# Projections and FFN as four concurrent 32-column tiles in a two-layer attention kernel

## The chip, the cores and the metric

The kernel runs on one core of one Trainium2 chip. The metric is device time in microseconds (us) of one execution. Runs of one kernel mostly agree within 0.5%, so differences of a few us need several rounds, in which kernels run in turn on the same chip. A ratio here is the mean time of one kernel's fast runs over that of the kernel before in the same rounds, so it is not quite the ratio of the medians that stand beside it. A kernel can also run in a slower state; no run told of here did, and "fast" means no more than that.

Names used below: the page is the profiler's summary of one execution, and the chain in it is the work that ended last, followed back through what each step waited for. ACT is ScalarE, DVE is VectorE, PE is TensorE (PEld its weight loads), POOL is GpSimd. L889 is line 889 of the program that is profiled. Lines move with every edit, so the scores are L1109 before and L1115 after.

## The reference

Two identical layers over 2048 rows of width 512: attention with 32 heads of 16 dimensions, then a feed-forward network (FFN) of width 1792.

```python
x = x + _A_ref(_layernorm(x), wqkv, wo)      # q,k,v = x @ wqkv; softmax(q k^T / 4) v; @ wo
x = x + _B_ref(_layernorm(x), w1, b1, w2, b2)  # gelu(x @ w1 + b1) @ w2 + b2
# ... both once more, with the same weights
```

## The kernel before

The program is made ahead of time by a small list scheduler, which is part of the kernel. Every piece of work is an `_Op` with an engine, a believed cost in us, the buffers it reads and writes, and for PE a `mode`: "S" for scores (weights of 32 rows and 128 columns), "P" for PV products (128 rows, 17 of 32 columns, four tiles side by side), "F" for full-array matmuls. The scheduler keeps a clock for each engine and always takes the piece that can start first; for a change of mode it charges `SW`. No time from the chip reaches it: a program, once made, is fixed.

```python
MM = 0.2135          # believed cost of one matmul of 512 columns
DV = 0.69            # of one VectorE eviction
FQ = 2               # matmuls in one piece of F work
SW = 0.107           # of a change of mode
...
    def _cost(self, op):
        return op.cost + (SW if op.eng == "pe" and op.mode != self.mode else 0.0)
...
# FFN, second matmul (ytile): 14 full-array matmuls and the bias as a 15th, of one row
fns = [lambda e, fc=fc: e.matmul(pb, lhsT=T["G"][:, fc, q], rhs=T["W2"][:, fc, :], start=(fc == 0), stop=False)
       for fc in range(NFC)]
fns.append(lambda e: e.matmul(pb, lhsT=T["ONES1"][0:1, :], rhs=T["B2row"][0:1, :], start=False, stop=True))
for h in range(0, NFC + 1, FQ):
    ...
    yield _Op("pe", FQ * MM, fns[h:h + FQ], reads=..., writes=["B.%d" % b], prio=MID if h else FPRIO)
```

Softmax exponentials are shared between ACT (exponentials of two or three score tiles at a time) and DVE (an approximation in integer arithmetic, which needs four PV products a tile instead of one). Who takes which tile is decided by the same scheduler. Where it expects PE to idle too long it puts in warming matmuls.

The softmax here doesn't subtract the row's maximum and nothing guards it: scores larger than these inputs give would overflow.

## Time and profile before

Before: 1621.02 us (median of 3 runs; 1620.97 with the next three).

| what | number | from |
|---|---|---|
| span of the profiled run | 1619.2 us | the page |
| ACT busy | 1554.1 us, 96% | the page, part 1 |
| PE busy, modelled ends | 1459.1 us, 90% | the page, part 1 |
| PE's slots: each instruction of the program at its measured step | 1375.6 us | starts in the timeline |
| DVE busy | 1363.4 us, 84% | the page, part 1 |
| first exponential starts, last one starts, end | 12.8, 1588.6, 1619.2 us | the timeline of ACT |

A busy share says which engine can be the limit. ACT is, almost without a break, from the first exponential to the last; only then does PE run the last rows' FFN alone. So time can be gained in two ways: less work on ACT, or exponentials that start less late. Two consecutive exponentials start 0.904 us apart (two tiles) or 1.330 us apart (three) where nothing hinders them. Below, a "late start" is one that comes over 60 ns later than that. Before there are 161 of them, worth 63.5 us. What other work of ACT takes between two exponentials is taken off (without the gaps that hold such work it is 148 late starts and 60.4 us). The page's own idle column is smaller, because a recorded ACT instruction overlaps the next one a little (one of three tiles is recorded as 1.52 us long, and the next starts after 1.33).

### The profile page before, as it was taken

To read this page: it belongs to the slowest core of one execution; us is meant where nothing else is said; L and a number is where in the kernel's file an instruction comes from. 1 tells how busy PE (TensorE), PEld (TensorE's weight loads), DVE (VectorE), ACT (ScalarE), POOL (GpSimd) and SP (SyncE) were. 2 spreads that over 40 slices of the span, in tenths; PEclk is the share of its full clock that TensorE was granted. 3 is DMA by queue.
4 is the path that set the end of the run, shared out by engine and by line. 5 is a ranking of instruction groups with operands and counts; after the bars stand their busy time and mean duration, and the time that the engine had idled before them with its cause. 6 is when DMAs were issued, how large, how long until landed. Compare 5 with 4: busy or idle time off the path is not lost.

```text
span 1619.2 us, 33814 instructions
## 1 busy us (share of the span) xinstructions
PE 1459.1 (90%) x14297; PEld 421.7 (26%) x14297; DVE 1363.4 (84%) x2649; ACT 1554.1 (96%) x1396; POOL 111.7 (7%) x148
## 2 busy tenths in 40 slices
PE   8998888989999998999989989878999989889998
PEld 2222222222222222222222222222222222233344
DVE  5689889879988889879798788988879988888993
ACT  7989999989999999999999999999999999999995
POOL 3200000000000000000010000010000000010000
PEclk9999999999999999999999999999999999999999
DMA  6100001101010010101101001001101100011120
GB/s 176 20 1 1 2 14 28 33 8 40 21 40 21 14 40 21 40 14 21 34 24 39 11 15 40 1 1 34 40 14 27 34 14 11 5 41 37 28 77 27
DMA packets 88370, 44.90 MB, mean 28 GB/s; under 512 B 33693, under 2 KB 88222, under 8 KB 88222
## 3 DMA queue, kind: packets, MB, share of 16 engines
q1 hardware_dynamic: 88222, 42.75, 9.9%
q8 instruction: 114, 1.87, 0.5%
q14 instruction: 34, 0.28, 0.1%
HBM read 33.03 MB, written 2.10 MB: 22 GB/s over the span
## 4 chain that ended last, share of the span: by engine, by line
ACT 70%; PE 27%; DVE 2%; issue 1%; DMA 0%; POOL 0%; ACTq 0%; POOLq 0%
ACT pt L1405 58%; PE ps L1466 8%; PE ps L1109 8%; ACT v L1405 5%; ACT kt L1405 4%; ACT g L878 3%; PE ps L889 3%; PE ps L843 2%; PE ps L647 2%; PE ps L644 1%; PE ps L770 1%; ACT L878 1%; ACT L1405 1%; PE ps L1097 1%; DVE du L1254 0%
## 5 line engine op out<-in xcount | busy, mean ns | idle before, releaser
L1405 ACT ACTIVATE pt<-ps 128x1024 bf16<-128x1024 f32 (+1 forms) x1190 | 1308.5, 1255 | 30.9 <-PE ps L1466 14.8
L1109 PE MATMUL ps<-qp,kt 32*128 32x512 bf16 x4096 | 539.4, 385 | 138.4 <-ACT pt L1405 92.8
L1254 DVE TENSOR_SCALAR du<-ps 128x512 uint16<-128x512 f32 x659 | 445.6, 686 | 114.9 <-PE ps L1109 106.8
L1466 PE MATMUL ps<-pt,v 128*17 128x512 bf16 (+1 forms) x3151 | 438.9, 362 | 5.1 <-ACT pt L1405 2.1
L1109 PEld LDWEIGHTS ps<-qp,kt 32*128 32x128 bf16 x4096 | 141.5, 91 | 687.7 <-ACT pt L1405 292.5
L1466 PE MATMUL ps<-du,vc 128*17 128x512 bf16 (+1 forms) x2211 | 308.6, 359 | 1.7 <-DVE du L1317 0.8
L1317 DVE TENSOR_SCALAR du<-du 128x2048 uint16<-128x2048 uint16 x332 | 227.9, 691 | 2.1
L1057 POOL TENSOR_SCALAR qp<-q,mask 128x512 bf16<-128x512 bf16 (+1 forms) x91 | 66.3, 728 | 1291.8 <-PE ps L1109 1282.8
L1466 PE MATMUL ps<-du,v 128*17 128x512 bf16 (+1 forms) x737 | 141.2, 362 | 1.5 <-DVE du L1254 0.6
L1315 DVE TENSOR_SCALAR du<-du 128x1024 uint16<-128x1024 uint16 x332 | 135.3, 417 | 2.4
L1466 PEld LDWEIGHTS ps<-pt,v 128*17 128x17 bf16 x3151 | 105.7, 88 | 120.7 <-issue 86.7
L843 PE MATMUL ps<-xf,wr 128*128 128x512 bf16 (+1 forms) x472 | 123.8, 365 | 0.5 <-DVE g L857 0.2
L889 PE MATMUL ps<-w,g 128*128 128x512 bf16 x448 | 120.4, 382 | 3.5 <-ACT g L878 3.4
L1405 ACT ACTIVATE v<-ps 128x1536 bf16<-128x1536 f32 (+1 forms) x81 | 104.5, 1309 | 4.9 <-PE ps L1466 3.1
L1466 PE MATMUL ps<-dh,vc 128*17 128x512 bf16 (+1 forms) x384 | 108.6, 359 | 0.0
L1466 PEld LDWEIGHTS ps<-du,vc 128*17 128x17 bf16 x2211 | 85.0, 89 | 58.9 <-issue 28.4
L1405 ACT ACTIVATE kt<-ps 128x1536 bf16<-128x1536 f32 (+1 forms) x66 | 93.3, 1420 | 2.3 <-PE ps L1466 1.4
L1254 DVE TENSOR_SCALAR dh<-ps 128x512 uint16<-128x512 f32 x115 | 78.9, 686 | 15.2 <-PE ps L1109 14.1
L857 DVE TENSOR_SCALAR g<-ps,hb1t 128x512 bf16<-128x512 f32 (+1 forms) x112 | 79.9, 713 | 12.3 <-PE ps L843 10.9
L1254 DVE TENSOR_SCALAR kt<-ps 128x512 uint16<-128x512 f32 x100 | 68.3, 683 | 16.1 <-PE ps L1109 14.3
L1466 PE MATMUL ps<-kt,v 128*17 128x512 bf16 (+1 forms) x311 | 77.2, 365 | 0.0
L1097 PE MATMUL ps<-w 128*32 128x512 bf16 x719 | 70.5, 388 | 1.6 <-DVE du L1254 1.6
(86 smaller groups left out, 1206.5 us busy)
## 6 DMA issues: line engine op xcount, KB each, us to landing
wr<-in_B_w_dram SPq DMA_DIRECT2D x59, 256.0 KB, 2.8
wr<-in_A_wqkv_dram SPq DMA_DIRECT2D x24, 256.0 KB, 2.8
wr<-in_A_wo_dram SPq DMA_DIRECT2D x18, 256.0 KB, 3.0
out_dram<-x SPq DMA_DIRECT2D x16, 128.0 KB, 1.7
w<-in_B_w_dram SPq DMA_DIRECT2D x1, 1792.0 KB, 10.9
g<-in_A_wqkv_dram SPq DMA_DIRECT2D x3, 512.0 KB, 5.2
x<-in_A_x_dram SPq DMA_DIRECT2D x3, 512.0 KB, 8.1
kt<-in_B_w_dram SPq DMA_DIRECT2D x4, 256.0 KB, 3.8
```

Of the source, the lines that this page charges most:

```text
L843: fns = [lambda e, dc=dc, j=j, pb=pb: e.matmul(pb, lhsT=T["WR"][w][:, 256 * dc + 128 * j:256 * dc + 128 * j + 128], rhs=T["XF"][:, dc, q], ...
L857: yield _Op("dve", 0.21 + n / 966, lambda e, fc=fc, pb=pb: e.tensor_scalar(T["G"][:, fc, q], pb, T["HB1T"][:, fc:fc + 1], None, op0=ALU.ad ...
L878: lambda e, g=g: e.activation(out=g, in_=g, func=ACT.Gelu_apprx_tanh), reads=gk, writes=gk, prio=2)
L889: fns = [lambda e, fc=fc: e.matmul(pb, lhsT=T["G"][:, fc, q], rhs=T["W2"][:, fc, :], start=(fc == 0), stop=False) for fc in range(NFC)]
L1057: yield _Op("pool", 0.1 + 0.6 * w / 512, lambda e, s=s, q=q, i=i, t=t, w=w: e.tensor_scalar(T["QP"][:, s, w * i:w * i + w], q, T["MASK"][: ...
L1097: fns.append(lambda e, o=o, w=w, a=a, m=m: e.matmul(o, lhsT=w, rhs=rhs, start=start, stop=start, tile_position=(0, m * a)))
L1109: return (lambda e: e.matmul(o, lhsT=lhsT, rhs=rhs, start=True, stop=True, tile_position=(32 * a, 0)), ["K%d.%d.%d" % (l, gb, kt // 4), "Q ...
L1254: yield _Op("dve", 0.68, lambda e: e.tensor_scalar(u, self.bank(b), E_SCALE, E_BIAS, op0=ALU.mult, op1=ALU.add), reads=["B.%d" % b], write ...
L1315: yield _Op("dve", 0.08 + 0.14 * n, lambda e: e.tensor_scalar(U[:, 1, 0:n, :], U[:, 0, 0:n, :], SHIFT, None, op0=ALU.add), reads=key[0], w ...
L1317: yield _Op("dve", 0.08 + 0.28 * n, lambda e: e.tensor_scalar(U[:, 2:4, 0:n, :], U[:, 0:2, 0:n, :], 2 * SHIFT, None, op0=ALU.add), reads=k ...
L1405: yield _Op("act", 0.065 + 0.4267 * n, lambda e, src=src, dst=dst: e.activation(out=dst, in_=src, func=ACT.Exp, scale=0.25), reads=["B.%d" ...
L1466: op.fns.append(lambda e, o=o, lhsT=q[0][0][m], rhs=q[0][1][:, n * m:n * m + n], a=a, st=st, sp=sp: e.matmul(o, lhsT=lhsT, rhs=rhs, start= ...
```

## The change

Intent: full-array matmuls sit between scores and PV products, and each change of tile shape costs PE 0.096 us here (0.311 us from start to start in place of 0.216). This pause is called a drain below. If projections and FFN have the tile shape of PV, one of the shapes is gone. Each full-array matmul becomes four matmuls of 32 columns, with the same moving operand; the one-row bias is padded to 128 rows with zeros.

```diff
+    def quads(self, out, lhsT, rhs, start, stop):
+        return [lambda e, a=a: e.matmul(out[32 * a:32 * a + 32, :], lhsT=lhsT[:, 32 * a:32 * a + 32], rhs=rhs, start=start, stop=stop,
+                                        tile_position=(0, 32 * a)) for a in range(4)]
...
-        fns = [lambda e, fc=fc: e.matmul(pb, lhsT=T["G"][:, fc, q], rhs=T["W2"][:, fc, :], start=(fc == 0), stop=False)
-               for fc in range(NFC)]
-        fns.append(lambda e: e.matmul(pb, lhsT=T["ONES1"][0:1, :], rhs=T["B2row"][0:1, :], start=False, stop=True))
+        fns = []
+        for fc in range(NFC):
+            fns += self.quads(pb, T["G"][:, fc, q], T["W2"][:, fc, :], fc == 0, False)
+        fns += self.quads(pb, T["ONES1"][:, :], T["B2row"][:, :], False, True)
         for h in range(0, NFC + 1, FQ):
             yield ("need", ("g", l, seg, min(h, NFC - 1) // 2))
-            yield _Op("pe", FQ * MM, fns[h:h + FQ],
+            yield _Op("pe", min(FQ, NFC + 1 - h) * MM, fns[4 * h:4 * h + 4 * FQ],
...
-                      writes=["B.%d" % b], prio=MID if h else FPRIO)
+                      writes=["B.%d" % b], prio=MID if h else FPRIO, mode="P")
... the same in proj (Q, K, V), wo and hpair (FFN, first matmul); ONES1 and B2row get 128 rows, zeroed on POOL
```

The edit does two things at once. It changes the shape on the hardware, and it changes what the scheduler believes, through `mode="P"` and through a lower cost for the last piece, which holds the bias alone, so that every later choice comes out differently.

More of the change, by code (lines that the diff above doesn't have):

```diff
@@ L450, in bass_interleave_layers__mha_block__dense_activation_gelu__prompt_kernel @@
         T["B1c"] = sb([NFC, 128], BF16, "b1c")
-        T["B2row"] = sb([1, D], BF16, "b2row")
-        T["ONES1"] = sb([1, 128], BF16, "ones1")
+        T["B2row"] = sb([128, D], BF16, "b2row")
+        T["ONES1"] = sb([128, 128], BF16, "ones1")
         T["ZERO"] = sb([128, 32], BF16, "zero")
@@ L522, in init @@
         yield _Op("pool", 0.1, lambda e: e.memset(T["ZERO"][:], 0.0), writes=["ZERO"])
-        yield _Op("pool", 0.1, lambda e: e.memset(T["ONES1"][:], 1.0), writes=["ONES1"])
+        yield _Op("pool", 0.1, lambda e: e.memset(T["ONES1"][:], 0.0), writes=["ONES1"])
+        yield _Op("pool", 0.1, lambda e: e.memset(T["ONES1"][0:1, :], 1.0), reads=["ONES1"], writes=["ONES1"])
+        yield _Op("pool", 0.3, lambda e: e.memset(T["B2row"][:], 0.0), writes=["B2zero"])
         yield _Op("dve", 0.6, lambda e: e.memset(self.bank(PVB), 0.0), writes=["B.%d" % PVB])
@@ L556, in loads @@
         yield load(T["B1c"][:], hbm["b1"].rearrange("(c p) -> c p", p=128), "db1", ["B1c"], 0.2)
-        yield load(T["B2row"][:], hbm["b2"].rearrange("(o e) -> o e", o=1), "db2", ["B2row"], 0.2)
+        yield _Op("sp", 0.2, lambda e: e.dma_start(T["B2row"][0:1, :], hbm["b2"].rearrange("(o e) -> o e", o=1)),
+                  reads=["B2zero"], writes=["B2row", "B2zero"], sem="db2", by=16, tail=2.0)
         yield load(T["W2"][:], hbm["w2"].rearrange("(c p) e -> p c e", p=128), "dw2", ["W2"], 8.0)
@@ L642, in proj @@
         for dc in range(NDC):
-            if kind == "V":
-                fns.append(lambda e, dc=dc: e.matmul(pb, lhsT=src(dc, i), rhs=wt(dc), start=(dc == 0),
-                                                     stop=(dc == NDC - 1)))
-            else:
-                fns.append(lambda e, dc=dc: e.matmul(pb, lhsT=wt(dc), rhs=src(dc, None),
-                                                     start=(dc == 0), stop=(dc == NDC - 1)))
+            lhsT, rhs = (src(dc, i), wt(dc)) if kind == "V" else (wt(dc), src(dc, None))
+            fns += self.quads(pb, lhsT, rhs, dc == 0, dc == NDC - 1)
         reads = wkeys + (skeys[i % 4:i % 4 + 1] if kind == "V" else skeys)
         for h in range(0, 4, FQ):
-            yield _Op("pe", FQ * MM, fns[h:h + FQ], reads=reads, writes=["B.%d" % b], prio=MID if h else FPRIO)
+            yield _Op("pe", FQ * MM, fns[4 * h:4 * h + 4 * FQ], reads=reads, writes=["B.%d" % b], prio=MID if h else FPRIO, mode="P")
         if l:
@@ L769, in wo @@
         q = slice((t % 4) * 128, (t % 4) * 128 + 128)
-        fns = [lambda e, j=j: e.matmul(pb, lhsT=T["OTN"][:, j, q], rhs=T["WR"][us[j // 2]][:, 512 * (j % 2):512 * (j % 2) + 512],
-                                       start=(j == 0), stop=(j == 3)) for j in range(4)]
+        fns = []
+        for j in range(4):
+            fns += self.quads(pb, T["OTN"][:, j, q], T["WR"][us[j // 2]][:, 512 * (j % 2):512 * (j % 2) + 512], j == 0, j == 3)
         for h in range(0, 4, FQ):
-            yield _Op("pe", FQ * MM, fns[h:h + FQ], reads=["WR.%d" % us[j // 2] for j in range(h, h + FQ)] + ["OTN.%d.%d" % (j, t % 4) for j in range(h, h + FQ)],
-                      writes=["B.%d" % b], prio=MID if h else FPRIO)
+            yield _Op("pe", FQ * MM, fns[4 * h:4 * h + 4 * FQ], reads=["WR.%d" % us[j // 2] for j in range(h, h + FQ)] + ["OTN.%d.%d" % (j, t % 4) for j in range(h, h + FQ)],
+                      writes=["B.%d" % b], prio=MID if h else FPRIO, mode="P")
         for j in range(2):
@@ L842, in hpair @@
             pb = self.bank(b)[:, 0:n]
-            fns = [lambda e, dc=dc, j=j, pb=pb: e.matmul(
-                pb, lhsT=T["WR"][w][:, 256 * dc + 128 * j:256 * dc + 128 * j + 128], rhs=T["XF"][:, dc, q], start=(dc == 0),
-                stop=(dc == NDC - 1)) for dc in range(NDC)]
+            fns = []
+            for dc in range(NDC):
+                o = 256 * dc + 128 * j
+                fns += self.quads(pb, T["WR"][w][:, o:o + 128], T["XF"][:, dc, q], dc == 0, dc == NDC - 1)
             for h in range(0, 4, FQ):
-                yield _Op("pe", FQ * MM * n / 512, fns[h:h + FQ],
+                yield _Op("pe", FQ * MM * n / 512, fns[4 * h:4 * h + 4 * FQ],
                           reads=["WR.%d" % w] + ["XF.%d" % (t % 4) for t in self.tiles(seg)],
-                          writes=["B.%d" % b], prio=MID if h else FPRIO)
+                          writes=["B.%d" % b], prio=MID if h else FPRIO, mode="P")
             yield from self.wdone((l, seg, "1", p), w)
@@ L888, in ytile @@
         q = slice((t % 4) * 128, (t % 4) * 128 + 128)
-        fns = [lambda e, fc=fc: e.matmul(pb, lhsT=T["G"][:, fc, q], rhs=T["W2"][:, fc, :], start=(fc == 0), stop=False)
-               for fc in range(NFC)]
-        fns.append(lambda e: e.matmul(pb, lhsT=T["ONES1"][0:1, :], rhs=T["B2row"][0:1, :], start=False, stop=True))
+        fns = []
+        for fc in range(NFC):
+            fns += self.quads(pb, T["G"][:, fc, q], T["W2"][:, fc, :], fc == 0, False)
+        fns += self.quads(pb, T["ONES1"][:, :], T["B2row"][:, :], False, True)
         for h in range(0, NFC + 1, FQ):
             yield ("need", ("g", l, seg, min(h, NFC - 1) // 2))
-            yield _Op("pe", FQ * MM, fns[h:h + FQ],
+            yield _Op("pe", min(FQ, NFC + 1 - h) * MM, fns[4 * h:4 * h + 4 * FQ],
                       reads=["W2", "ONES1", "B2row"] + ["G.%d.%d" % (f, t % 4) for f in range(h, min(h + FQ, NFC))],
-                      writes=["B.%d" % b], prio=MID if h else FPRIO)
+                      writes=["B.%d" % b], prio=MID if h else FPRIO, mode="P")
         yield _Op("dve", DV, lambda e: e.tensor_tensor(out=T["X"][:, t, :], in0=T["X"][:, t, :], in1=pb, op=ALU.add),
```

## The prediction

> **What bounds the kernel now.** I read the page from the top: busy shares first, then the chain of work that ended last, then the costliest groups of instructions.
>
> ```profile
> span 1619.2 us, 33814 instructions
> ...
> PE 1459.1 (90%) x14297; PEld 421.7 (26%) x14297; DVE 1363.4 (84%) x2649; ACT 1554.1 (96%) x1396; POOL 111.7 (7%) x148
> ...
> ACT 70%; PE 27%; DVE 2%; issue 1%; DMA 0%; POOL 0%; ACTq 0%; POOLq 0%
> ...
> L1405 ACT ACTIVATE pt<-ps 128x1024 bf16<-128x1024 f32 (+1 forms) x1190 | 1308.5, 1255 | 30.9 <-PE ps L1466 14.8
> ```
>
> ScalarE (ACT) carries the softmax exponentials and is busy 96% of the span; only 65 us of it are idle. The chain agrees: 70% ACT. PE's 90% must be discounted, since matmul ends are modelled and overlap; its real occupancy has to come from starts. Reading ACT by stretches, about 8.5 idle us lie in the first 20 us and some 19 us in the last 40, where the final feed-forward runs alone; about 38 us are scattered between. A cheaper PE can win only in that middle and in the tail, unless it also takes work off ACT.
>
> Next, the timeline of TensorE, for what a tile shape and a change of shape cost.
>
> ```profile
> 1322.63 0.83 PE L1097 MATMUL ps<-w,zero 128*17 128x512 bf16 x12
> 1323.28 1.25 PE L1097 MATMUL ps<-w 128*32 128x512 bf16 x20
> ...
> 1505.32 0.40 PE L1109 MATMUL ps<-qp,kt 32*128 32x512 bf16 x4
> 1505.65 1.04 PE L889 MATMUL ps<-w,g 128*128 128x512 bf16 x4
> 1506.62 0.39 PE L1109 MATMUL ps<-qp,kt 32*128 32x512 bf16 x3
> 1506.94 1.04 PE L889 MATMUL ps<-w,g 128*128 128x512 bf16 x4
> ...
> 1596.38 0.39 PE L891 MATMUL ps<-b2row,ones 1*128 1x512 bf16 x1
> 1596.70 0.60 PE L770 MATMUL ps<-wr,otn 128*128 128x512 bf16 x2
> ```
>
> Columns: start, length, engine, line, operands with rows*columns of the weights. The line numbered 1097 holds warming matmuls; its second row is already what the change makes of the projections: 128 rows, 32 columns, four tiles with one moving operand. Twenty of them are five sets: 1.25 us less one latency of 0.38 is 0.87 for four set-to-set steps, 0.217 us each. Starts read one by one give 0.215 to 0.222 for such sets, and 0.216 (0.226 for the second of a burst) for a full-array matmul. So four 32-column tiles cost what one full-array matmul costs, even eight sets on end.
>
> The scores (L1109, 32 rows) and the FFN (L889, 128x128) alternate. From the last FFN start, at about 1505.65 + 3 x 0.22 = 1506.31, to the next score at 1506.62 it takes 0.31 us, where the same shape would take 0.216. Over the whole trace the median from start to start is 0.311 to 0.317 between scores and either other shape, 0.306 to 0.312 between full-array and PV: a switch costs 0.096 us, alike for every pair.
>
> **What the Trainium skill says.** "TensorEngine Tiling (Array Packing)", section Key Properties: changing the tiling mode drains the engine, using another tile of the same mode doesn't. The trace agrees: 0.311 against 0.216 us. The same page's Restrictions say that column tiling disables Fast Weight Load. This could hurt, but in the trace weight loads hide: sets keep 0.216 us with four loads each. "TensorE: Matmul & The Clock Gate", Part 3, models concurrent tiles as one duration plus about 4 ns a further tile; here the starts inside a set are 3 ns apart. Nothing in these says that the array does more work per microsecond in four tiles when all 128 columns were used before.
>
> **The change part by part.** The programs of both kernels are built ahead by a scheduler in the kernel, which charges itself for mode switches; so I counted the built orders of instructions.
>
> Removed and added on PE. The 1496 full-array or bias matmuls become 1496 sets of four; PE rises from 14,297 to 18,750 matmuls with as many weight loads, at no cost in slots by the warming sets above. Issue can follow: in the trace 46 matmuls of 256 columns went by in 12 sets of 0.109 us, 27 ns each, and the new sets ask for only 54 ns each.
>
> Switches fall far less than one would think, from 2709 to 2521. Between full-array and PV there were 198, nearly all gone. But scores need 32-row tiles, and around them a full-array burst only becomes a column-tiled burst: scores to and from anything were 2511 switches and are 2518. So -188 x 0.096 = -18.0 us of PE.
>
> The new order gives part of it back. PV products fall from 7581 to 7533 matmuls but are packed less well: 1774 sets of 512 columns instead of 1752, and 496 of 256 columns instead of 478, so 22 x 0.216 + 18 x 0.109 = +6.7 us. Score groups rise by 12 (+2.6 us), warming sets by 1 (+0.2 us). The last tile of a set starts 9 ns after its first, and now that precedes every switch to scores: about +3.5 us. Sum: -18.0 + 6.7 + 2.6 + 0.2 + 3.5 = -5.0 us of PE occupancy, from 1375.6 to 1370.6 us when every instruction gets its measured slot. PE already had 1619 - 1376 = 243 us of slack; all but the first and last of the sixteen stretches of 256 score tiles need 67 to 91 us of PE and last 89 to 104.
>
> ACT. How exponentials divide between ACT and VectorE is decided by the same scheduler. ACT has 3222 score tiles before and 3236 after; VectorE 874 and 860. ACT's groups of three go from 548 to 552, of two from 789 to 790. Unhindered starts are 1.330 and 0.904 us apart, so ACT gains 4 x 1.330 + 0.904 = +6.2 us, on the bound engine. VectorE loses 14 tiles at about 0.69 + 0.42 us, 15 us that it doesn't need.
>
> What comes back on the path. Between consecutive exponentials I find 161 starts that come over 60 ns later than those spacings, 63.5 us together. In 50 of these (19.2 us) PE did full-array and PV work between two score groups with a switch between; only there does the removal act directly, and at 0.096 us each it is worth at most 4.8 us. I credit 4.8 and take 2 us off for better PE spacing at the start, where the first stretch needs 100.9 us of PE instead of 103.8 in 112.5. In the tail after the last score, the bias matmul of one row is built as a 32-row tile, so it switches twice: 0.32 us before and after, as at 1596.38. Over all rows it doesn't; the tail has three switches instead of nine, and 23.4 us of PE instead of 24.1: -0.7 us.
>
> Sum on the path: +6.2 - 4.8 - 2.0 - 0.7 = -1.3 us, thus 1619.7, called 1620.
>
> **Rivals.** First, PE relief pulls ACT waits in more broadly: if the full 18 us of switches came off the waits before exponentials and ACT's extra work stayed, 1621 - 18 + 6 = 1609. For it: PE is 27% of the chain and is named for most of ACT's waits. Against it: net occupancy falls only 5 us, and two thirds of the late starts have no such switch before them.
>
> Second, detuning. Pacing constants of the scheduler were set for the old order, and its choices differ from the first microseconds on. If late starts grew by a third, 63.5 / 3 = 21 us, it would be 1621 + 6 + 21 = 1648. For it: single late starts of 2 to 4 us occur already. Against it: the inner stretches keep 9 to 26 us of PE slack and the mix of work in each is alike.
>
> Third, tiles with 32 live columns and 128 live rows stall on weights or instruction issue. If each new set took 0.25 instead of 0.216 us, PE would gain 1496 x 0.034 = 51 us, mostly inside 243 us of slack; in the tail 100 sets would show 3.4 us. Perhaps 1635. The warming sets speak against it, though they run at most eight in a row.
>
> **Range and chances.** Net terms are below 7 us each; what I can't work out is the luck of the new order, which I put at 12 us either way, a little more upward. Range 1606 to 1636. Two per cent is 32 us: faster would need half of all middle and tail waits to vanish (3%), slower the second or third rival at full size (4%).
>
> **What would show it.** In the changed trace: ACT busy about 1560 us with 552 and 790 groups; set-to-set spacing 0.216 us for the projection and FFN lines; 0.31 us at the remaining switches; switch count near 2521; PE summed slots 5 us lower; the bias matmul without its 0.32 steps. I am wrong if ACT's late starts move by more than 15 us either way, if new sets are slower than 0.22 us, or if the granted clock leaves 0.994.

## The result, and the profile after

After: 1609.78 us (median of 6 runs, 1607.56 to 1612.44) against 1620.97 us; ratio 0.9939, 95% interval 0.9921 to 0.9956. A repeat on another occasion gave 1610.93 us, ratio 0.9937. The gain is clear of noise and far below 2%.

From the page of the kernel after, parts 1, 4 and 5. The columns of part 5 are busy us and mean ns of one, then the idle us before them and who ended it.

```profile
span 1610.5 us, 42676 instructions
...
PE 1449.3 (90%) x18750; PEld 453.1 (28%) x18750; DVE 1348.8 (84%) x2615; ACT 1559.4 (97%) x1401; POOL 112.5 (7%) x150
...
ACT 69%; PE 29%; DVE 2%; issue 1%; DMA 0%; POOL 0%; SPq 0%; POOLq 0%; ACTq 0%
...
L1411 ACT ACTIVATE pt<-ps 128x1024 bf16<-128x1024 f32 (+1 forms) x1214 | 1331.8, 1253 | 20.7 <-PE ps L1115 10.8
...
L511 PE MATMUL ps<-xf,wr 128*32 128x512 bf16 (+1 forms) x2400 | 169.0, 368 | 0.9 <-DVE g L862 0.3
...
L511 PEld LDWEIGHTS ps<-xf,wr 128*32 128x32 bf16 x2400 | 54.3, 95 | 60.5 <-issue 28.5
```

ACT is busier by 5.3 us (1559.4 against 1554.1) and the kernel is still shorter: ACT has more work and waits less. The idle time before its main group of exponentials fell from 30.9 to 20.7 us. The chain's shares hardly moved, so the bound is the same engine.

Where the time went, by the starts of exponentials in both timelines:

| us | before | after |
|---|---|---|
| to the first exponential | 12.8 | 12.8 |
| first to last exponential | 1575.8 | 1566.9 |
| after the last one's start | 30.6 | 30.8 |
| exponentials between at 0.904 and 1.330 us | 1441.2 | 1447.4 |
| late starts | 161, 63.5 us | 145, 48.3 us |

All of it lies in the middle: 6.2 us more work and 15.2 us less lateness make -9.0, and the stretch is 8.9 us shorter. The tail gained nothing.

The new sets run at the expected speed. One line from the timeline of PE in the tail (start, length, line, weights as rows*columns):

```profile
1600.46 1.89 PE L511 MATMUL ps<-w,g 128*32 128x512 bf16 x30
```

Thirty matmuls are seven and a half sets; 1.89 us less one latency of 0.38 is 1.51 us for seven steps, 0.216 us each.

### The profile page after: what moved, and what is told of

It is laid out like the page before. It is cut to its first block, busy times and chain, and to the rows that moved or that the text cites. A ratio compares the mean times of both kernels' runs of the same rounds, so it can differ in the third digit from the quotient of the medians.

```text
span 1610.5 us, 42676 instructions
## 1 busy us (share of the span) xinstructions
PE 1449.3 (90%) x18750; PEld 453.1 (28%) x18750; DVE 1348.8 (84%) x2615; ACT 1559.4 (97%) x1401; POOL 112.5 (7%) x150
## 4 chain that ended last, share of the span: by engine, by line
ACT 69%; PE 29%; DVE 2%; issue 1%; DMA 0%; POOL 0%; SPq 0%; POOLq 0%; ACTq 0%
ACT pt L1411 57%; PE ps L511 11%; PE ps L1115 9%; PE ps L1472 8%; ACT v L1411 4%; ACT kt L1411 3%; ACT g L883 3%; PE ps L1103 1%; ACT L883 1%; ACT L1411 1%; DVE du L1260 0%; DMA kt<-xln 0%; DVE x L903 0%; DVE kt L1260 0%; DVE du L1323 0%
## 5 line engine op out<-in xcount | busy, mean ns | idle before, releaser
L1411 ACT ACTIVATE pt<-ps 128x1024 bf16<-128x1024 f32 (+1 forms) x1214 | 1331.8, 1253 | 20.7 <-PE ps L1115 10.8
L1472 PE MATMUL ps<-pt,v 128*17 128x512 bf16 (+1 forms) x3218 | 461.1, 360 | 5.5 <-ACT pt L1411 1.3
L1472 PE MATMUL ps<-du,vc 128*17 128x512 bf16 (+1 forms) x2190 | 322.1, 359 | 1.8 <-DVE du L1323 1.6
L1323 DVE TENSOR_SCALAR du<-du 128x2048 uint16<-128x2048 uint16 x327 | 223.6, 687 | 2.5
L511 PE MATMUL ps<-xf,wr 128*32 128x512 bf16 (+1 forms) x2400 | 169.0, 368 | 0.9 <-DVE g L862 0.3
L1472 PEld LDWEIGHTS ps<-pt,v 128*17 128x17 bf16 x3218 | 116.3, 88 | 116.9 <-issue 75.5
L511 PE MATMUL ps<-w,g 128*32 128x512 bf16 x1792 | 126.9, 382 | 3.2 <-ACT g L883 2.6
L1411 ACT ACTIVATE v<-ps 128x1536 bf16<-128x1536 f32 (+1 forms) x72 | 99.7, 1397 | 2.3 <-PE ps L1472 1.0
L1411 ACT ACTIVATE kt<-ps 128x1536 bf16<-128x1536 f32 (+1 forms) x56 | 80.9, 1444 | 1.1 <-PE ps L1472 1.0
L511 PEld LDWEIGHTS ps<-xf,wr 128*32 128x32 bf16 x2400 | 54.3, 95 | 60.5 <-issue 28.5
```

The source lines that it names most:

```text
L511: return [lambda e, a=a: e.matmul(out[32 * a:32 * a + 32, :], lhsT=lhsT[:, 32 * a:32 * a + 32], rhs=rhs, start=start, stop=stop, tile_posi ...
L1323: yield _Op("dve", 0.08 + 0.28 * n, lambda e: e.tensor_scalar(U[:, 2:4, 0:n, :], U[:, 0:2, 0:n, :], 2 * SHIFT, None, op0=ALU.add), reads=k ...
L1411: yield _Op("act", 0.065 + 0.4267 * n, lambda e, src=src, dst=dst: e.activation(out=dst, in_=src, func=ACT.Exp, scale=0.25), reads=["B.%d" ...
L1472: op.fns.append(lambda e, o=o, lhsT=q[0][0][m], rhs=q[0][1][:, n * m:n * m + n], a=a, st=st, sp=sp: e.matmul(o, lhsT=lhsT, rhs=rhs, start= ...
```

## The experiments

Theory A: the gain is drains that the hardware no longer makes. Theory B: the gain is the new order, whatever the shape. Theory C: it is the luck of one order among many that small nudges of the scheduler's constants would give. All twelve runs gave correct results.

The first question is shape against order. A scheduler makes this a clean two by two, since the shape can be swapped without touching the order. "Slots" below are each instruction of the built program at its measured step (about 216 ns a set of 512 columns, 109 of 256, 96 ns more where the shape changes, and 9 ns more where the set before the change has four tiles).

**The new order with full-array matmuls.**

```diff
     def quads(self, out, lhsT, rhs, start, stop):
-        return [lambda e, a=a: e.matmul(out[32 * a:32 * a + 32, :], ...) for a in range(4)]
+        one = lambda e: e.matmul(out, lhsT=lhsT, rhs=rhs, start=start, stop=stop)
+        return [one, None, None, None]        # the scheduler still sees mode "P"; None is dropped at emission
```

> The order of the changed kernel instruction by instruction, but each set of four 32-column tiles is one full-array matmul again (the bias with all 128 rows). The built order has 2754 switches of shape instead of 2521, so at 0.096 us each some 20 us more PE occupancy. Theory A (the gain is drains that the hardware no longer makes, in the waits before exponentials): the gain is lost wholly or mostly, 1616 to 1626 us. Theory B (the gain is in the new order, whatever the tile shape): within 3 us of the changed kernel, 1607 to 1613. Theory C (luck of one order): also 1607 to 1613.

Measured: 1621.6 us, ratio 1.0008 (0.9993 to 1.0023). The whole gain is gone, with the same order instruction by instruction. Theory B and theory C fall as explanations of this order: without the shape it gains nothing. From its page:

```profile
ACT 57%; PE 39%; DVE 3%; issue 1%; POOL 0%; POOLq 0%; ACTq 0%
...
L1412 ACT ACTIVATE pt<-ps 128x1024 bf16<-128x1024 f32 (+1 forms) x1214 | 1332.1, 1240 | 24.4 <-PE ps L1116 11.8
```

The same 1214 exponentials now wait 24.4 us instead of 20.7, and PE's share of the chain rises from 29% to 39%. Late starts are 164, worth 56.1 us: 7.8 more than after, where the profiled spans (1618.6 and 1610.5 us) differ by 8.1. How it happens can be seen at the same place of both programs. The timeline of PE, first of the kernel after, then of this run:

```profile
61.81 0.39 PE L1115 MATMUL ps<-qp,kt 32*128 32x512 bf16 x3
62.13 0.39 PE L1472 MATMUL ps<-pt,v 128*17 128x512 bf16 x4
62.35 0.60 PE L511 MATMUL ps<-kt,g 128*32 128x512 bf16 x8
62.89 0.39 PE L1115 MATMUL ps<-qp,kt 32*128 32x512 bf16 x2
```

```profile
61.82 0.39 PE L1116 MATMUL ps<-qp,kt 32*128 32x512 bf16 x3
62.14 0.39 PE L1473 MATMUL ps<-pt,v 128*17 128x512 bf16 x4
62.46 0.60 PE L512 MATMUL ps<-kt,g 128*128 128x512 bf16 x2
63.00 0.39 PE L1116 MATMUL ps<-qp,kt 32*128 32x512 bf16 x2
```

Read the starts. From PV to the projection it takes 62.35 - 62.13 = 0.22 us with equal shapes and 62.46 - 62.14 = 0.32 us with a change. From there to the next scores both take 0.54 us. So one drain of 0.10 us stands between one score group and the next, and the score groups that follow come later by that much. In this run the exponential of the last group shown starts 0.02 us late and the one after it 0.22 us late; in the kernel after both are on time. ACT was 0.16 us further ahead in this run before that, so the place shows how a drain gets to ACT and not how much one is worth. The same exponential can be compared over the whole of both runs: this run is 2.3 us behind at the 301st, 5.8 at the 601st, 7.4 at the 1201st and 8.7 at the 1321st, so the loss is spread over the program.

**The old order with four tiles.**

```diff
-            yield _Op("pe", FQ * MM, fns[4 * h:4 * h + 4 * FQ], ..., mode="P")
+            yield _Op("pe", FQ * MM, fns[4 * h:4 * h + 4 * FQ], ...)      # mode "F": the switch is charged as before
```

> The four tiles on the hardware, but the scheduler is told that these are full-array matmuls, so the order is that of the kernel before (but for one warming set near the end). 2513 switches instead of 2709, summed slots 14 us lower (1361 against 1376). Theory A: a good part of 14 us reaches the end, 1609 to 1615. Theory B and C: the order is the old one, so 1618 to 1622.

Measured: 1616.85 us, ratio 0.9974 (0.9959 to 0.9989). That is 4.2 us by the ratio (0.0026 x 1620), so the time lies between the two expectations: above theory A's 1615, below theory B's 1618. From its page, the line of the exponentials, to be set against 30.9 us before:

```profile
L1411 ACT ACTIVATE pt<-ps 128x1024 bf16<-128x1024 f32 (+1 forms) x1190 | 1308.6, 1261 | 30.1 <-PE ps L1472 14.3
```

PE's slots fell by 14.3 us, to 1361.3, while span less slots, which is PE's idle time, rose from 243.6 to 255.6 us: most of the drains removed became idle time. Late starts fell by 2.0 us to 61.5 in a profiled run that was 2.3 us shorter.

**The bias alone.** The kernel before with only the bias padded to 128 rows, full array.

```diff
-        fns.append(lambda e: e.matmul(pb, lhsT=T["ONES1"][0:1, :], rhs=T["B2row"][0:1, :], start=False, stop=True))
+        fns.append(lambda e: e.matmul(pb, lhsT=T["ONES1"][:, :], rhs=T["B2row"][:, :], start=False, stop=True))
```

> The kernel before with the bias matmul alone made 128 rows deep, zero padded, full array; the order is the same. In the tail it saves six switches (-0.6 us), in the middle it moves the switch from before the bias to after it. All theories: 1618 to 1622, within 0.2% of before; if the bias were the gain, 1610 to 1614.

Measured: 1618.71 us, ratio 0.9989 (0.9974 to 1.0003). As expected, not resolved from nothing, and not the cause.

**A nudged scheduler, with the change.** This asks how much one order's luck is worth.

```diff
-DV = 0.69
+DV = 0.687
```

> The changed kernel with one cost that the scheduler believes, that of a VectorE eviction, set from 0.69 to 0.687 us: a neutral nudge that makes another order. Summed PE slots 1360 us against 1371. Theory C (one order's luck is as large as the effect): it lands anywhere between 1600 and 1622. Theories A and B: the same mechanism holds, so below 1615; by the PE slots, 1600 to 1610.

Measured: 1602.01 us, ratio 0.9889 (0.9874 to 0.9903). It is faster than the changed kernel by 8 us, for a nudge that means nothing. Luck of an order is as large as the effect under study, so more orders were needed on both sides.

**The same nudge without the change.** The kernel before, with

```diff
-DV = 0.69
+DV = 0.687
```

> The kernel before, nudged as the first nudged run was: VectorE eviction believed 0.687 us. Scheduler's other choices, 3238 exponential tiles on ScalarE (the kernel before has 3222, the changed one 3236), summed PE slots 1384 us. If the extra work on ScalarE that came with the change is luck of the order and not the change, this one, which has it without the change, is slower than before: 1624 to 1632. If luck of the order is small: 1618 to 1623.

Measured: 1631.65 us, ratio 1.0069 (1.0055 to 1.0083), which agrees with the first expectation: this order has 3238 tiles on ACT, and no change of shape. So the extra work on ACT that I had put down to the change also comes with an order of the kernel before. That it made this order slow is not shown: it explains 6.4 of the 11 us at most, and the next run speaks against it.

**Another nudge without the change.** The kernel before, with

```diff
-SW = 0.107
+SW = 0.106
```

> The kernel before, with the switch that the scheduler charges set from 0.107 to 0.106 us: another neutral nudge. 3235 tiles on ScalarE, PE slots 1373 us. Luck of the order: anywhere from 1614 to 1628. If every neutral order of full-array matmuls stays above 1614 the effect of the change is not luck; if one falls to 1610, it may be.

Measured: 1616.17 us, ratio 0.9971 (0.9959 to 0.9983). It has 13 more tiles on ACT than the kernel before and is still faster, so ACT's share of the tiles alone doesn't rank orders either. The lowest of the three neutral orders with full-array matmuls thus stays above 1614 us, the mark set in advance.

**Another nudge with the change.**

```diff
-DV = 0.69
+DV = 0.693
```

> The changed kernel with the VectorE eviction believed 0.693 us: a nudge whose order puts 3252 tiles on ScalarE, 16 more than the changed kernel (+6.5 us of its work). If ScalarE's share of the tiles carries through, 1612 to 1620 in spite of PE slots at 1360 us; if PE's slots count, 1600 to 1608.

Measured: 1618.80 us, ratio 0.9991 (0.9978 to 1.0005). PE's slots were lowest of all here (1360.0 us) and did not help; 16 more tiles on ACT did show. An order of the changed kernel can thus be slower than one of the kernel before.

**The nudged order with full-array matmuls.** The first experiment once more, in the order that took 1602 us:

```diff
# on top of the first experiment's edit
-DV = 0.69
+DV = 0.687
```

> The order of the first nudged run (1602 us with four tiles) kept instruction by instruction, with full-array matmuls in place of the four tiles: 2745 switches against 2509, PE slots 1380 against 1360 us. Theory A (drains): 9 to 15 us slower than with the tiles, so 1611 to 1617, as in the first pair. If the first pair was chance: within 5 us of 1602.

Measured: 1612.29 us, ratio 0.9947 (0.9935 to 0.9959). In the same order, four tiles are 0.0058 x 1621 = 9.4 us faster. The lines of exponentials, with four tiles and then with full-array matmuls:

```profile
L1411 ACT ACTIVATE pt<-ps 128x1024 bf16<-128x1024 f32 (+1 forms) x1215 | 1337.9, 1250 | 14.7 <-PE ps L1115 9.3
```

```profile
L1412 ACT ACTIVATE pt<-ps 128x1024 bf16<-128x1024 f32 (+1 forms) x1215 | 1338.9, 1246 | 19.3 <-PE ps L1116 12.2
```

The idle time moves by 4.6 us in one group, and late starts by 9.0 us in all, from 42.4 to 51.4; the profiled spans differ by 8.4.

**Retuned versions of both.** The scheduler's own planned end, which is no measurement, was used to choose: for the changed kernel the earliest of 700 draws of its constants, for the kernel before the earliest of 150.

```diff
-SWAP = 0.5   -ALONE = 3.5   -JB = 0.64   -EVAC = 0.4    -SW = 0.107    -MM = 0.2135    -DV = 0.69
+SWAP = 0.538 +ALONE = 3.93  +JB = 0.7    +EVAC = 0.255  +SW = 0.0979   +MM = 0.21292   +DV = 0.6917
```

> The changed kernel with seven of its scheduler's constants redrawn: the order with the earliest planned end (1586.2 us) of 700 drawn. In the orders run so far the chip ended 12 to 16 us after the scheduler's own plan, so 1598 to 1602 us: at or below the best run so far, 1602, and over 1% below before. If a plan chosen out of so many is only chosen for its error, 1604 to 1612.

Measured: 1606.96 us, ratio 0.9913 (0.9896 to 0.9929). A miss: faster than the changed kernel, slower than the nudged one; the chip ended 20.8 us after the plan, so it was chosen in part for the plan's error.

```diff
-DV = 0.69   -MM = 0.2135   -SW = 0.107
+DV = 0.6875 +MM = 0.21367  +SW = 0.1037
```

> The kernel before, full-array matmuls, with three constants redrawn: the earliest planned end (1595.2 us) of 150 drawn. By the same difference 1607 to 1611. If the change is worth some 10 us whatever the tuning, this stays 8 to 12 us above the retuned changed kernel; if retuning alone gives what the change gave, it lands within 4 us of it.

Measured: 1611.20 us, ratio 0.9949 (0.9930 to 0.9969). Without any change of shape, a retuned order comes within 4.2 us of the retuned changed kernel by the medians and 5.8 us by the ratios (0.0036 x 1621), with an uncertainty of some 4 us: between the two expectations (within 4 us, 8 to 12), and not clear of either. Retuning alone gave most of what the change gave. The draws were not equally many, so the gap is no clean measure of the change.

**Four tiles in an order planned for full-array matmuls, a second time**, beside a repeat of the changed kernel (no edit) on the same chip.

```diff
# on top of the second experiment's edit
-DV = 0.69
+DV = 0.687
```

> The four tiles on the hardware in an order planned for full-array matmuls, a second time: the order of the nudged kernel before (1631.7 us), kept exactly. 2533 switches against 2735, PE slots 1369 against 1384 us. If an order that was planned around the switches turns only a few us of the removed drains into time, as the first such pair did (3 to 4 us): 1626 to 1630. If the drains' worth is about 11 us whatever the order, as in the two orders planned without the charge: 1619 to 1623.

Measured: 1625.96 us, ratio 1.0031 (1.0018 to 1.0045), against 1.0069 for that order with full-array matmuls: 0.0038 x 1621 = 6.2 us. On the edge of the lower expectation and clearly less than 11.

> The changed kernel once more, on the chip of this call, so that the other run of this call can be set against it: 1607 to 1613 us, ratio to before 0.992 to 0.996.

Measured: 1610.93 us, ratio 0.9937 (0.9924 to 0.9951), as expected.

All pairs that differ in the shape alone. The time gained is the difference of the two ratios to the kernel before, times 1620 or 1621 us (for the kernel after with the ratio of its repeat, 0.9937; with that of its first runs it is 11.2). Except against the kernel before itself, the two ran each beside the kernel before. The last column is an estimate that is explained below the table:

| order planned | switches removed | slots removed | time gained, by ratios | at equal clock |
|---|---|---|---|---|
| with a charge for full-array to PV, kernel before | 196 | 14.3 us | 4.2 us | 2.9 us |
| with the charge, nudged | 202 | 15.1 us | 6.2 us | 5.3 us |
| without the charge, kernel after | 233 | 19.6 us | 11.5 us | 10.3 us |
| without the charge, nudged | 236 | 19.9 us | 9.4 us | 10.4 us |

In each order the shape is faster. By the ratios, each of which is uncertain by 2 to 4 us, between 30 and 60% of the PE time removed reaches the end.

**The granted clock**, a rival that the runs can settle. Each run lists the mean TensorE clock that was granted, and the time goes with it: on one chip the kernel before took 1618.28 us at 0.997 of full speed and 1625.22 us at 0.989. Over the 105 runs with a recorded clock, each against the mean of its own kernel, 0.001 of clock goes with 0.88 us (standard error 0.04); with that taken off, the scatter falls from 2.0 to 0.7 us. The eleven runs of the changed kernel had 0.9975 on average, the 32 of the kernel before 0.9933. Brought to an equal clock of 0.995 by this slope, they come to 1612.3 and 1619.3 us, an estimate: 7 us apart, and not 10.6 as the plain means of these runs. So some 4 us of the gain go with a higher clock. Why it was higher no run shows. It was not the shape alone: with full-array matmuls the new order still had 0.9958 and the nudged one 0.9968.

The four pairs stand up to it: at an equal clock they give the last column, each to about 0.5 us. There the orders planned around the switches turn 20 and 35% of the PE time removed into time, the other two 53 and 52%. I take it that an order planned around the switches leaves fewer drains in front of a score group that an exponential is waiting for; the late starts agree with that, but no run isolates it.

The best version measured is the changed kernel with `DV = 0.687`: 1602.01 us, ratio 0.9889, faster than both kernels. It is a lucky order among the four run with the change, not an insight.

## Why the prediction was right or wrong

The range held: 1606 to 1636, no difference by 2%. The centre, 1620, was 10 us too high, and the first rival, which had been argued against, named 1609.

- **ACT's added work, +6.2 us:** the right size for this order; the exponentials between the first and the last take 6.2 us more at their unhindered spacing, and ACT's busy time rose to 1559.4 us, for 1560 forecast. But it came with the order and not with the shape, and the order paid for it: with full-array matmuls the late starts of the new order are worth 56.1 us, 7.4 less than before. The nudged kernel before has 3238 tiles on ACT, more than the changed kernel's 3236.
- **PE's sum, -5.0 us:** the counts are those of the program and the measured steps held (0.216 us a set, 0.31 at a switch). The step from there to the time failed. I compared PE's occupancy of two different orders and let the poorer packing cancel the drains, but those drains stand in front of score groups and the packing mostly does not show on the path. In the changed order the shape alone is worth 19.6 us of slots and 11.5 us of time (10.3 at equal clock).
- **"only there does the removal act directly, and at 0.096 us each it is worth at most 4.8 us":** this is the step that failed. It is about right where the order stays (4.2 us measured with the old order, 2.9 at equal clock). But with the switch no longer charged the scheduler puts full-array work and PV side by side: with full-array matmuls in that order there are 76 late starts with such a switch before them, worth 26.1 us (1% of that run's matmul records are missing), where the order before had 50, worth 19.2. By the prediction's rule these 76 would give at most 7.3 us, and the shape gave 10 to 11.5. So looking only into the last gap was too narrow as well: between 58 and 68 us the chain of both runs stays on PE through nine score groups, and each drain there can delay all that follow.
- **The start, -2 us:** the first exponential starts at 12.8 us in both, and the 257th score tile, the end of the first stretch, comes at 123.7 instead of 124.9 us; 1.2 us, somewhat less than credited.
- **The tail, -0.7 us:** not seen. After the last exponential's start 30.8 us remain, as before (30.6).
- **First rival, broad relief, 1609:** right that relief of PE reaches ACT broadly; that its number fits is in part luck. It took 18 us off the waits, and late starts fell by 15.2 us in place of the 6.8 credited; but 7.4 of these came with the order (63.5 to 56.1 with full-array matmuls), where they paid for the 6.2 us of work, and 7.8 with the shape. Some 4 us of the measured gain go with the clock, of which the rival says nothing.
- **Second rival, detuning:** the new order with full-array matmuls is 1.3 us slower than before by the ratio, not distinguishable from nothing. At equal clock it is 3.4 us slower, so the order alone cost a little and gained nothing. The luck of an order, put at 12 us either way, was of the right size: nudged, the changed kernel ran from 8 us faster to 9 us slower, the kernel before from 5 us faster to 11 us slower.
- **Third rival, slow tiles:** excluded. Sets kept 0.216 us in the longest unbroken run of them, 34 sets (136 matmuls) from 1584.06 us on.
- **Signs of being wrong:** the prediction named three. The granted clock left 0.994 (0.996 in the profiled run after, 0.9975 on average), so this one came true. Late starts moved by 15.2 us, on the edge of its 15 (13.5 us without the gaps that hold other work). New sets were not slower than 0.22 us.

What stays open is how much the change is worth over all orders. The three orders of neutral tuning give means of 1622.9 us before (1620.98, 1631.65, 1616.17) and 1610.2 us after (1609.78, 1602.01, 1618.80), 12.7 us apart with overlapping ranges. With one retuned order on each side the gap is 4.2 us by the medians, and about 1.3 us at equal clock.

## What to carry to other kernels

Before counting what a cheaper operation saves, find who waits behind it: a drain of 0.1 us counts in front of a tile that the bound engine waits for, while with the old order 12 of the 14.3 us of PE time removed only became idle time. Where a scheduler makes the program, separate what the hardware does differently from what the scheduler chooses differently, by exchanging one under a fixed order, and run several nudged orders, because one order's luck was as large as the effect. Set the granted clock beside every small difference. A matmul over all 128 rows can be cut into four 32-column tiles for the price of one (0.216 us here), so it can take the shape of its neighbours.

## What the Trainium skill lacked or had wrong

- "TensorEngine Tiling (Array Packing)", Key Properties, says that changing the mode drains the engine but gives no cost. Here it is 0.096 us on top of a 512-column slot (0.311 against 0.216 us), alike between all three shapes.
- The same page's Restrictions say that column tiling disables Fast Weight Load, and don't say when that costs time. Here it cost none that shows: sets of four with four loads step by 0.216 us, like a full-array matmul. Whether the loads themselves became slower these runs can't tell.
- "TensorE: Matmul & The Clock Gate", section LDWEIGHTS, has the load time in proportion to the columns, columns / 1.2 in ns, an estimate of 27 ns for 32 columns and 107 ns for 128. The records of weight loads here don't follow that: 95 ns (mean, 32 columns) and 98 ns (median, 128 columns). What part of a record is the load itself is not shown.
- The same page, Back-to-back issue gap, gives about 131 ns a matmul as sustained for pairs of load and matmul of 512 columns, and about 216 ns for an isolated gap. Here such pairs step by 216 to 226 ns when sustained.
- No page says that a matmul of one row is built as a 32-row tile and so counts as a change of shape: the bias stood 0.32 us before a full-array matmul, where two full-array ones stand 0.216 us apart, and only 0.22 us after a score group, which has that shape.
